# A third tensor of batch 0 (q of heads 2 and 3) through the hardware queue as fp32 rows, cast on chip, with the start's order planned anew

## The chip, the cores and the metric

The kernel runs on one core of one Trainium2 chip. The metric is the device time of one execution in microseconds (us), as the median of several runs; lower is better. The profile is one execution recorded by the hardware profiler.

In the names of the engines, PE is TensorE (matmuls; PEld is its weight load), ACT is ScalarE, DVE is VectorE, POOL is GpSimd and SP is SyncE. POOL and SP start DMA transfers: those of POOL go through the software queue (q0 in the profile) and can change the type on the way, those of SP go through the hardware queue (q1) and copy as is. All of them are moved by the core's 16 DMA engines.

## The reference

Two operations, one after the other. First a causal attention with a sliding window of 64 positions, then a feed-forward layer with SiLU:

```python
# q, k, v: (8, 8, 576, 64) float32;  w_in: (512, 2048), w_out: (2048, 512)
scores = (q @ k.transpose(0, 1, 3, 2)) / 8          # head_dim 64
mask = (rel >= 0) & (rel < 64)                      # rel = row - column
attn = softmax(where(mask, scores, -1e9))
x = (attn @ v).transpose(0, 2, 1, 3).reshape(4608, 512)
h = x @ w_in
out = (h * sigmoid(h)) @ w_out                      # (4608, 512) float32
```

## The kernel before, in words

**The work.** Inputs are loaded once and turned to bf16. The attention is done batch by batch (8 batches). Its result goes, transposed, into a tile `bridge`. The feed-forward part works on 9 tiles of 512 tokens: a first layer (L369, out of `bridge` and `w_in_sb`), SiLU on ACT (L375, into tiles `g`), a second layer (L381, out of `g` and `w_out_sb`), a copy out of PSUM (L387) and a store by SP (L391). The first tile, j = 0, is widened to 576 columns, all of batch 0. Its first layer is done in passes: for the feature blocks ft 0 to 7 the columns 0 to 191 (128x192 matmuls), then for the same blocks the columns 192 to 575 (128x384), then ft 8 to 15 in two pieces each.

**Batch 0** has a way of its own, in `add_first_batch`. There are 8 loads of q and k, each of two heads (a *pair* u), in the order of `FIRST_LOADS`: q0 k0 q1 k1 q2 q3 k2 k3. So q1 is the q of heads 2 and 3. Each of them lies in DRAM as 128 rows of 2304 B.

- q0 and k0 come by `load_first` (L232): SP moves 288 KB of fp32 rows into a tile `nat`, and ACT or DVE then casts them into a tile `natb` (`cast_first`, L235).
- The other six come by `load_first_cast` (L229): POOL issues a DMA that casts on the way, 144 KB into `natb`.
- When two pairs of one tensor are there, PE turns them with 18 transposes (`turn_first`, L282) into two PSUM banks, and ACT and DVE lift them into `qt` and `kt` (L289).
- Then come scores with the mask as a bias (L311, L319), exp on ACT (L337), values (L349), a reciprocal (L356), a product (L359) and a transpose into `bridge` (L363) on DVE. There are six such units: three groups g of 192 columns for each half a of the heads. v arrives by POOL (L253), and half of each v tile is shifted to other partitions (L297, L299).

While PE has nothing else to do at the start it runs filler matmuls on an empty tile (`warm`, L595).

**The order.** A planner, `Plan.run`, walks through an event simulation with a cost for every operation, and fixes one order of instructions for every engine at build time. On the chip each engine goes through its own list and waits on semaphores; nothing is reordered. Costs of DMAs enter as `dma=...`: there are two pipes in the planner, one for SP and one for POOL, with a slowdown when both are busy.

**The queues.** POOL's list at the start is: four of the six casting loads, the constant `ident` (L188), the other two, the constant `window` (L193, L195), four v loads (L253), ten loads of w_in (L259: four of 256 columns, then six of 512, in pairs of two row halves), and then, mixed, the rows of batch 1 (L239), w_out (eight loads, L265) and v of batch 1. Every DMA of POOL waits for the one eight before it to have landed, since its semaphores are used in turn. SP's list is q0 and k0, and then nothing until the first store, after 51 us.

**What waits for the weights.** A block ft of the first layer needs its columns of w_in: ft 0 and 1 the first pair of loads, 2 and 3 the second, 4 to 7 the third, and so on. The second layer of tile 0 goes f by f, and f needs w_out load f // 2.

Of the kernel before, what the change touches and what calls it, by code (L numbers as in the profile page):

```python
# [8 lines left out]
FP32 = mybir.dt.float32  # L9
# [5 lines left out]
class Plan:  # L15
# [31 lines left out]
    def run(self):  # L47
        head = {c: 0 for c in self.queues}
        engines = sorted({e for q in self.queues.values() for op in q for e in op["us"]})
        free = {e: 0.0 for e in engines}  # L50
        can = {e: [c for c, q in self.queues.items() if any(e in op["us"] for op in q)] for e in engines}
        table, left = "exp", self.count
        pipe, sent = {True: 2.0, False: 0.0}, []
        events, order = [0.0], []
        while left:
            if not events:
                raise RuntimeError([(c, head[c], q[head[c]]["n"]) for c, q in self.queues.items() if head[c] < len(q)])
            now = self.now = heapq.heappop(events)
            while events and events[0] == now:
                heapq.heappop(events)  # L60
            moved = True
            while moved:
                moved = False
                for e in engines:
                    if free[e] > now:
                        continue
                    best, kept = None, set()
                    heads = [(self.queues[c][head[c]], c) for c in can[e] if head[c] < len(self.queues[c])]
                    for op, c in sorted(heads, key=lambda x: x[0]["first"]):
                        if e == "POOL" and op["dma"] and len(sent) >= 8 and sent[-8] > now:  # L70
                            continue
                        if e not in op["us"] or not self.done(op["deps"]) or (op["gate"] and not op["gate"]()):
                            continue
                        if op["pool"]:
                            idle = [i for i in self.pools[op["pool"]] if i not in kept and self.done(self.banks[i])]
                            if len(idle) < len(op["untils"]):
                                if op["pool"] != "mp":
                                    kept.update(self.pools[op["pool"]])
                                continue
                            idle.sort(key=lambda i: (op["pool"] == "mp" and i in self.pools["pv"],  # L80
                                                     max([u["seen"] for u in self.banks[i]], default=0.0)))
                            op["bank"] = idle[:len(op["untils"])]
                            for i, until in zip(op["bank"], op["untils"]):
                                self.banks[i] = until
                        best = (op, c)
                        break
                    if best is None:
                        continue
                    op, c = best
                    head[c] += 1  # L90
                    us = op["us"][e]
                    if op["table"] and op["table"] != table:
                        table, us = op["table"], us + 1.28
                    end = free[e] = now + us
                    soft = e == "POOL"
                    if op["dma"] is None:
                        op["seen"] = end + op["lat"]
                    elif soft:

                        begin = max(pipe[True], end + 1.4)  # L100
                        pipe[True] = begin + op["dma"] * (1.5 if pipe[False] > begin else 1.0)
                        op["seen"] = pipe[True] + op["lat"] + 1.2
                        sent.append(op["seen"])
                        heapq.heappush(events, op["seen"])
                    else:
                        begin = max(pipe[False], end + 1.0)
                        busy = pipe[True] > begin
                        pipe[False] = begin + op["dma"] * (1.6 if busy else 1.0)
                        if busy:
                            pipe[True] += 0.6 * op["dma"]  # L110
                        op["seen"] = pipe[False] + {"ld0": 1.2, "st": 1.2}.get(c, 3.0)
                    op["at"], op["cls"], op["by"] = now, c, e
                    order.append((op, e))
                    left -= c != "warm"
                    moved = True
                    heapq.heappush(events, end)
                    heapq.heappush(events, op["seen"])
        for op, e in order:
            op["fn"](e)
# [3 lines left out]
def kernel(ctx, tc, q, k, v, w_in, w_out, out):  # L123
    nc = tc.nc
    B, H, S, D = q.shape
# [13 lines left out]
    FIRST_LOADS = [(x[0], int(x[1])) for x in "q0 k0 q1 k1 q2 q3 k2 k3 v0 v1 v2 v3".split()]  # L139
# [20 lines left out]
    nats = [keep.tile([128, 2 * S], BF16, name=f"nat{i}") for i in range(NN)]  # L160
# [15 lines left out]
    p = Plan(  # L176
        {"at": range(4), "pv": range(4, 6), "mp": range(4, 8), "all": range(8)},
        rank=dict(prime=-8, early=-10, one=-9, edge=-8.5, first=-9, dma=-1, ld0=-1, dma0=-8.7, st=-2, silu=-3, out=-2, pv=0, s=1, moe=99, warm=200, turn=2,
                  norm=0, inverse=0, bridge=0, exp=1, mask=1, lift=2, block=2, shift=2, cast=4, rest=3, late=5, clear=9),
        rank0=dict(turn=-6, cast=-6, lift=-5, shift=-4.5, exp=-4, mask=-4, inverse=-3.5, norm=-3, bridge=-3.2),  # L180
        ahead=dict(s=-5.5, exp=-4.6, pv=-5.5, inverse=-4.3, norm=-4.2, bridge=-4.25),
    )
# [42 lines left out]
    def two(u, kk):  # L225
        return (q, k)[kk][0, 2 * u:2 * u + 2].rearrange("h s d -> (h s) d").rearrange("(p m) d -> p (m d)", m=NM0)

    def load_first_cast(w, u, kk):
        nc.gpsimd.dma_start(out=natbs[w][:, 0:S], in_=two(u, kk))  # L229

    def load_first(i, kk):
        nc.sync.dma_start(out=nats[i][:, 0:2 * S].bitcast(FP32), in_=two(0, kk))  # L232

    def cast_first(e, i, w):
        copies[e](out=natbs[w][:, 0:S], in_=nats[i][:, 0:2 * S].bitcast(FP32))  # L235
# [178 lines left out]
    def add_first_batch():  # L414
        got = {}
        for what, u in FIRST_LOADS:
            if what == "v":
                add_v_loads(0, [u], [c_vv[0]])
                continue
            kk = "qk".index(what)  # L420
            w = n_nat[1] % NNB
            n_nat[1] += 1
            if u == 0:
                i = n_nat[0] % NN
                n_nat[0] += 1
                ld = p.add("ld0", {"SP": 0.45}, lambda _, i=i, kk=kk: load_first(i, kk), dma=-0.15 if kk == 0 else 0.7)
                ca = p.add("cast", {"ACT": 0.7, "DVE": 0.56}, lambda e, i=i, w=w: cast_first(e, i, w), [ld])
                nat_free[i] = [ca]
            else:
                ca = p.add("early" if (what, u) in FIRST_LOADS[2:6] else "dma0", {"POOL": 0.6}, lambda _, w=w, u=u, kk=kk: load_first_cast(w, u, kk), dma=0.74)  # L430
            got[what, u] = (w, ca)
            if (what, u ^ 1) not in got:
                continue
            a = u // 2
            ws, loaded = zip(*[got[what, 2 * a + i] for i in range(2)])
            tu = p.add("turn", {"PE": 0.6}, None, [*loaded, c_ident], lat=0.1, pool="all", nb=2)
            tu["fn"] = lambda _, tu=tu, ws=ws: turn_first(tu, ws)
            for i in range(2):
                tu["untils"][i].append(p.add("lift", {"ACT": 0.64, "DVE": 0.75}, lambda e, tu=tu, a=a, kk=kk, i=i:
                                             lift(e, tu, a, kk, i), [tu, c_k[0]]))  # L440
                kq_done[(0, a)] = kq_done.get((0, a), []) + tu["untils"][i]
# [23 lines left out]
    def add_v_loads(b, parts, busy):  # L465
        v_landed.setdefault(b, []).extend(
            p.add("dma", {"POOL": 1.0}, lambda e, part=part: load_v(e, b, part), busy, dma=1.0 if b == 0 else 1.1, lat=MARGIN * (b > 0)) for part in parts)
# [120 lines left out]


    add_first_batch()  # L590
    add_batch_v(0)

# [59 lines left out]
```

The softmax here doesn't subtract the row's maximum and nothing guards it: scores larger than these inputs give would overflow.

## Time and profile before

| what | value |
|---|---|
| time, median of 7 runs | 299.8 us (299.47 to 301.85) |
| profiled execution: its own time | 299.47 us |
| profiled execution: span | 297.7 us |
| PE busy | 286.4 us (96%), 3609 matmuls |
| ACT, DVE, POOL busy | 176.4, 138.3, 117.8 us |
| software queue q0 | 18.07 MB, 65.5% of the 16 DMA engines' span |
| hardware queue q1 | 10.03 MB, 9.5% |
| granted TensorE clock | 1.0 |

So 1.77 us of the profiled execution's own time lie outside its span. The other view that matters is the timeline, which lists instructions in order of time: start, duration, engine, line, operation, tiles, count, and in brackets how long the engine was idle before and what released it. Consecutive instructions of one kind are merged. The DMA view gives for each kind of DMA the KB and the median time from issue to landing. The chain of waits is followed back from the last instruction, and a piece of it that says "DMA" is a stretch in which nothing but that transfer set the time.

### The profile page before, as it was taken

The numbers are of one execution on the slowest core, as the hardware profiler recorded it, in microseconds if no ns is written. First come the engines' busy times: TensorE is split into PE (matmuls) and PEld (weight loads), VectorE is DVE, ScalarE is ACT, GpSimd is POOL, SyncE is SP. The second block draws the span as 40 slices with busy tenths as digits, with TensorE's granted clock in tenths as the row PEclk, the third lists the DMA queues.
The fourth block names the chain that finished last, engine by engine and source line by source line (L and its number), as shares of the span: only waits on it lengthen the run. The fifth ranks groups of instructions, "written<-read, shape, count | busy, mean of one in ns | idle before, by whom it ended". The sixth has DMA issues, their size and how long they took to land.

```text
span 297.7 us, 8484 instructions
## 1 busy us (share of the span) xinstructions
PE 286.4 (96%) x3609; PEld 149.3 (50%) x3641; DVE 138.3 (46%) x340; ACT 176.4 (59%) x340; POOL 117.8 (40%) x175
## 2 busy tenths in 40 slices
PE   8979989899999999999999999999999999999996
PEld 4556645774444544454444544454444544444445
DVE  3772378969985479327931692066006610000000
ACT  4878655786376745675477537743876376216512
POOL 8967976879799989940500000000000000000000
PEclk9999999999999999999999999999999999999999
DMA  8999999999999999982950210011001100010012
GB/s 163 173 201 175 146 166 169 233 121 137 181 165 140 129 178 177 149 84 75 105 48 0 75 53 20 2 40 70 35 0 40 73 35 2 35 72 35 2 70 72
DMA packets 82982, 28.64 MB, mean 96 GB/s; under 512 B 72448, under 2 KB 78208, under 8 KB 82944
## 3 DMA queue, kind: packets, MB, share of 16 engines
q0 software_dynamic: 77184, 18.07, 65.5%
q1 hardware_dynamic: 5760, 10.03, 9.5%
q8 instruction: 28, 0.46, 0.6%
q14 instruction: 10, 0.08, 0.1%
HBM read 36.70 MB, written 9.44 MB: 155 GB/s over the span
## 4 chain that ended last, share of the span: by engine, by line
PE 82%; POOL 8%; DMA 5%; issue 2%; ACT 1%; POOLq 0%; ACTq 0%
PE mp L381 39%; PE mp L369 37%; PE at L331 3%; PE mp L349 3%; DMA w_in_sb<-in_moe_w_in_dram 3%; DMA w_out_sb<-in_moe_w_out_dram 2%; POOL w_in_sb L259 2%; POOL nat L239 2%; POOL vv L253 2%; POOL natb L229 1%; POOL w_out_sb L265 1%; ACT ot L387 0%; ACT g L375 0%; PE at L349 0%; POOL window L193 0%
## 5 line engine op out<-in xcount | busy, mean ns | idle before, releaser
L369 PE MATMUL mp<-bridge,w_in_sb 128*128 128x512 bf16 (+5 forms) x696 | 128.6, 342 | 2.6 <-DMA w_in_sb<-in_moe_w_in_dram 1.0
L381 PE MATMUL mp<-w_out_sb,g 128*128 128x512 bf16 (+2 forms) x576 | 124.3, 367 | 4.5 <-issue 3.2
L375 ACT ACTIVATE g<-mp 128x512 bf16<-128x512 f32 (+5 forms) x174 | 89.6, 524 | 31.5 <-PE mp L369 30.3
L369 PEld LDWEIGHTS <-w_in_sb 128*128 128x128 bf16 x696 | 66.2, 97 | 63.1 <-issue 7.3
L381 PEld LDWEIGHTS <-g 128*128 128x128 bf16 x608 | 56.0, 98 | 61.9 <-issue 1.4
L387 ACT COPY ot<-mp 128x512 f32<-128x512 f32 (+2 forms) x36 | 20.2, 564 | 62.1 <-PE mp L381 42.8
L340 DVE TENSOR_TENSOR e<-e,mask 128x384 bf16<-128x384 bf16 x84 | 26.0, 347 | 49.1 <-ACT e L337 48.6
L337 ACT ACTIVATE e<-at 128x384 bf16<-128x384 f32 x90 | 37.3, 496 | 16.2 <-PE at L331 16.0
L239 POOL DMA_DIRECT2D nat<-in_k_dram x56 | 35.2, 643 | 8.3 <-DMA vv<-in_v_dram 3.9
L253 POOL DMA_DIRECT2D vv<-in_v_dram x32 | 31.9, 1013 | 14.8 <-PE mp L349 13.3
L239 POOL DMA_DIRECT2D nat<-in_q_dram x56 | 34.5, 632 | 4.4 <-DMA w_in_sb<-in_moe_w_in_dram 1.6
L363 DVE STREAM_TRANSPOSE bridge<-ox 128x384 bf16<-128x384 bf16 x48 | 24.7, 552 | 0.0
L246 DVE STREAM_TRANSPOSE kt<-nat 128x576 bf16<-128x576 bf16 x28 | 20.7, 782 | 6.0 <-DMA nat<-in_k_dram 6.0
L246 DVE STREAM_TRANSPOSE qt<-nat 128x576 bf16<-128x576 bf16 x28 | 20.9, 786 | 3.7 <-DMA nat<-in_q_dram 3.4
L359 DVE TENSOR_TENSOR ox<-mp,rc 128x384 bf16<-128x384 f32 x43 | 21.4, 537 | 0.1
L356 DVE RECIPROCAL rc<-mp 128x6 f32<-128x6 f32 x43 | 7.9, 189 | 18.5 <-PE mp L349 17.7
L349 PEld LDWEIGHTS <-e 128*32 128x32 bf16 x1152 | 10.9, 95 | 9.0 <-issue 5.1
L299 DVE COPY vv<-vv 64x576 bf16<-64x576 bf16 (+1 forms) x14 | 7.3, 523 | 14.0 <-DMA vv<-in_v_dram 11.2
L349 PE MATMUL mp<-vv,e 128*32 128x65 bf16 x1032 | 12.6, 194 | 0.2 <-ACT e L337 0.2
L331 PE MATMUL at<-qt,kt 32*128 32x64 bf16 x1008 | 11.6, 190 | 0.0
L331 PEld LDWEIGHTS <-kt 32*128 32x128 bf16 x1008 | 9.3, 92 | 4.3 <-issue 3.3
L337 ACT ACT_TABLE_LOAD x7 | 9.0, 1283 | 0.1
(53 smaller groups left out, 84.3 us busy)
## 6 DMA issues: line engine op xcount, KB each, us to landing
out_dram<-ot SPq DMA_DIRECT2D x35, 256.0 KB, 2.1
vv<-in_v_dram POOLq DMA_DIRECT2D x32, 144.0 KB, 5.1
nat<-in_q_dram POOLq DMA_DIRECT2D x56, 72.0 KB, 3.9
nat<-in_k_dram POOLq DMA_DIRECT2D x56, 72.0 KB, 3.9
w_out_sb<-in_moe_w_out_dram POOLq DMA_DIRECT2D x8, 256.0 KB, 6.6
w_in_sb<-in_moe_w_in_dram POOLq DMA_DIRECT2D x6, 256.0 KB, 7.6
w_in_sb<-in_moe_w_in_dram POOLq DMA_DIRECT2D x4, 128.0 KB, 5.1
natb<-in_q_dram POOLq DMA_DIRECT2D x3, 144.0 KB, 5.1
```

The lines of the kernel that those rows point to most:

```text
L239: nc.gpsimd.dma_start(out=nats[i][32 * h:32 * h + 32].rearrange("p (m x) -> p m x", m=NB), in_=(q, k)[kk][b, 4 * a + h].rearrange("(m p r) ...
L246: nc.vector.transpose(out=to[:, (2 * a + part) * S:(2 * a + part + 1) * S].rearrange("x (m t r) -> x m r t", t=32, r=2), in_=nats[i].rearr ...
L253: queue[e].dma_start(out=vv[b % NV][:, 2 * g0 + 1:2 * g1 + 1:2, 0:D], in_=v[b].rearrange("h s d -> (h s) d").rearrange("(g p) d -> p g d", ...
L331: nc.tensor.matmul(at_six(op["bank"][h])[:, a, x], lhsT=kt[b % NK][r, at:at + 128], rhs=qt[b % NK][r, at:at + 64], start=(s == a == x == 0 ...
L337: nc.scalar.activation(out=es[n % NE], in_=at_six(bank), func=ACTF.Exp, scale=scale)
L340: nc.vector.tensor_mul(es[n % NE], es[n % NE], mask0 if g == 0 else mask)
L349: nc.tensor.matmul(at_pv(bank)[32 * h:32 * h + 32, x, t], lhsT=e_of(b, a, n, h)[:, x, 32 * t:32 * t + 32], rhs=vv[b % NV][:, (4 * a + h) * ...
L359: nc.vector.tensor_mul(oxs[n % NOX], at_pv(bank)[:, :, :, 0:D], rcs[n % NRC].unsqueeze(3).to_broadcast([128, 3, 2, D]))
L363: nc.vector.transpose(out=bridge[:, n0:n0 + 3, 2 * a:2 * a + 2].rearrange("x t s (u i) -> x t s u i", u=2), in_=oxs[n % NOX].rearrange("p ...
L369: nc.tensor.matmul(banks[bank["bank"][0]][:, 0:hi - lo], lhsT=w_in_sb[:, c, ft * 128:(ft + 1) * 128], rhs=bridge[:, (j * TT + lo) // 64:(j ...
L375: nc.scalar.activation(out=gts[gt][:, lo:hi], in_=banks[bank["bank"][0]][:, 0:hi - lo], func=ACTF.Silu)
L381: nc.tensor.matmul(banks[bank["bank"][0]][:, 0:hi - lo], lhsT=gts[gt][:, m * 128:(m + 1) * 128], rhs=w_out_sb[:, f, lo:hi], start=(f == 0) ...
```

## The change

The load of q1 (q, heads 2 and 3, batch 0) is taken from POOL and given to SP: `load_first` gets the pair u as an argument, and the first three entries of `FIRST_LOADS` take that way. The transfer is now 288 KB of fp32 into a `nat` tile, and a cast by ACT or DVE comes behind it. The class "early", which puts four casting loads ahead of `ident` in POOL's list, moves on by one entry, and now holds k1, q2, q3, k2. The planner's costs for loads of the class `ld0` change too: 0.69 each in place of -0.15 and 0.7, no slowdown beside POOL's transfers, and 0.5 us in place of 1.2 from the end of the transfer to its being seen.

```diff
                         begin = max(pipe[False], end + 1.0)
-                        busy = pipe[True] > begin
+                        busy = pipe[True] > begin and c != "ld0"
...
-                        op["seen"] = pipe[False] + {"ld0": 1.2, "st": 1.2}.get(c, 3.0)
+                        op["seen"] = pipe[False] + {"ld0": 0.5, "st": 1.2}.get(c, 3.0)
...
-    def load_first(i, kk):
-        nc.sync.dma_start(out=nats[i][:, 0:2 * S].bitcast(FP32), in_=two(0, kk))
+    def load_first(i, u, kk):
+        nc.sync.dma_start(out=nats[i][:, 0:2 * S].bitcast(FP32), in_=two(u, kk))
...
-            if u == 0:
+            if (what, u) in FIRST_LOADS[0:3]:
...
-                ld = p.add("ld0", {"SP": 0.45}, lambda _, i=i, kk=kk: load_first(i, kk), dma=-0.15 if kk == 0 else 0.7)
+                ld = p.add("ld0", {"SP": 0.45}, lambda _, i=i, u=u, kk=kk: load_first(i, u, kk), dma=0.69)
...
-                ca = p.add("early" if (what, u) in FIRST_LOADS[2:6] else "dma0", {"POOL": 0.6}, lambda _, w=w, u=u, kk=kk: load_first_cast(w, u, kk), dma=0.74)
+                ca = p.add("early" if (what, u) in FIRST_LOADS[3:7] else "dma0", {"POOL": 0.6}, lambda _, w=w, u=u, kk=kk: load_first_cast(w, u, kk), dma=0.74)
```

The two programs' lists, laid side by side, differ as follows.

- **SP:** q0, k0, q1 in place of q0, k0.
- **POOL:** k1, q2, q3, k2, `ident`, k3, `window` in place of q1, k1, q2, q3, `ident`, k2, k3, `window`. All that follows keeps its order and stands one place earlier.
- **PE:** 18 fillers before the first turn in place of 15; then the turns of q0/q1, k0/k1 and q2/q3 one after another, two fillers, and the turn of k2/k3, all ahead of the first scores. Before, one filler stood behind the first turn and four behind the second, and the first unit of scores stood ahead of the turn of k2/k3. The six units of scores now come as (g0, a0), (g1, a0), (g0, a1), (g2, a0), two units of values, and the last two. From the first matmul of the first layer on, the list is the same but for the numbers of the PSUM banks.
- **ACT:** a third cast (q1) behind the two, and all four of its lifts ahead of the first exp. Before, three stood there and the fourth between the second and third exp.
- **DVE:** the two mask constants (L206) ahead of the first lift; the product of the second unit ahead of that of (g0, a1). Its later list is the same.

The tiles `nat` that batch 1 and later ones take are one further round the ring of eight.

## The prediction

> **What bounds the kernel now.** I read the page first: PE is busy in nearly every slice of the span, at full clock, and the DMA row is full only at the start.
>
> ```profile
> PE   8979989899999999999999999999999999999996
> PEclk9999999999999999999999999999999999999999
> DMA  8999999999999999982950210011001100010012
> ```
>
> So the time is PE's fixed work plus the gaps in it, and an edit of the start counts only through gaps. The chain of waits says which: until PE takes over at 42.27 us the chain consists of POOL's issues and of two waits for weights.
>
> ```profile
> 5.51 3.95 POOL vv L253 x4
> 9.46 4.12 POOL w_in_sb L259 x6
> ...
> 14.43 1.39 POOL w_in_sb L259 x2
> 15.82 9.00 DMA w_in_sb<-in_moe_w_in_dram
> ...
> 35.47 6.76 DMA w_out_sb<-in_moe_w_out_dram
> 42.23 0.04 issue
> 42.27 1.02 PE mp L381 x4
> ```
>
> The timeline of PE shows the gaps themselves: the first layer starts at 16.33, waits 0.40 for `bridge`, 0.97 for the third pair of w_in loads (until 19.76), then runs without a gap to the second layer, which waits 0.42 and 0.36 for w_out.
>
> ```profile
> 16.33 0.34 PE L369 MATMUL mp<-bridge,w_in_sb 128*128 128x192 bf16 x2
> 17.07 1.73 PE L369 MATMUL mp<-bridge,w_in_sb 128*128 128x192 bf16 x16 [0.40 <-DVE bridge L363]
> 19.76 14.37 PE L369 MATMUL mp<-bridge,w_in_sb 128*128 128x192 bf16 x110 [0.97 <-DMA w_in_sb<-in_moe_w_in_dram]
> ...
> 40.03 1.89 PE L381 MATMUL mp<-w_out_sb,g 128*128 128x512 bf16 x8 [0.42 <-DMA w_out_sb<-in_moe_w_out_dram]
> 42.27 1.02 PE L381 MATMUL mp<-w_out_sb,g 128*128 128x512 bf16 x4 [0.36 <-DMA w_out_sb<-in_moe_w_out_dram]
> ```
>
> Two chains thus meet. The **weights' stream** (POOL's DMAs in their order) sets 19.76 and 42.27. The **attention's start** (loads, turns, exps, 16.33) has 0.97 us of slack against it, and 0.42 + 0.36 = 0.78 more before the end of the kernel feels it. Is the stream held by POOL's issuing or by the DMA engines? POOL's timeline answers:
>
> ```profile
> 9.38 7.15 POOL L259 DMA_DIRECT2D w_in_sb<-in_moe_w_in_dram  x10
> 16.52 1.26 POOL L239 DMA_DIRECT2D nat<-in_q_dram  x2
> 18.26 0.61 POOL L239 DMA_DIRECT2D nat<-in_q_dram  x1 [0.48 <-DMA w_in_sb<-in_moe_w_in_dram]
> 20.00 0.60 POOL L239 DMA_DIRECT2D nat<-in_q_dram  x1 [1.13 <-DMA w_in_sb<-in_moe_w_in_dram]
> ```
>
> It never waits until 16.5, then waits at each DMA for the eighth one before to land: from there the engines hold it. Earlier, the time from issue to landing tells: 3.9 us for the first casting load, 4.9 to 5.4 for the other five, 5.2 to 6.0 for v, 5.1 for the small w_in loads, up to 9.0 for the last. Since a 72 KB load in an idle stretch later lands 2.8 us after its issue, something like 1.4 us of transfers is queued from k1 on. The engines bind nearly from the start, at the rates of these rows (busy shares of the engines, then clock, DMA share and GB/s, counted in bytes written):
>
> ```profile
> 3.00:4.00 1.00, 1.00 (x5) 0.50 (x4) 0.00 (x0) 0.33 (x1) 0.94 (x4) 1.00 1.07 345
> 5.00:6.00 1.00, 1.00 (x18) 0.55 (x17) 0.46 (x2) 0.15 (x1) 0.93 (x3) 1.00 1.04 149
> 7.00:8.00 1.00, 1.00 (x21) 0.70 (x17) 0.75 (x2) 0.64 (x1) 1.00 (x2) 1.00 1.16 177
> ```
>
> **The change, part by part.**
>
> *The stream, removed and added.* POOL loses one issue of 0.56 us. The engines lose a casting load of 147 KB written (295 KB read) and get 295 KB of fp32. In finer slices the hardware queue alone runs at 378 to 396 GB/s between 2.5 and 3.5 us, so 295 KB take about 0.75 us; the casting stream runs at 177, so 147 KB take 0.83 us (the landings of k1 at 6.8 and k3 at 9.8 give 0.75 each). Difference: between 0 and -0.08 us. There may be a little more: at 5 to 6 us the stream is at 149 only, 0.16 us of transfer below the later rate, which a second queue may fill. I take -0.1 us.
>
> Two rules of the Trainium skill bear on this, both in "DMA: Bandwidth & Descriptors". Its section "Issuing engines are not separate DMA queues" speaks against the change: DMAs of all engines run on the same 16 engines, and another issuer saves only the issue. Taken by itself this allows POOL's 0.56 us, all of it if issuing bound. The backlog above says that it doesn't: the ring's wait for the eighth DMA before gives the 0.56 back, since w_in load 7 already stands within 0.1 us of the landing that it waits for (v2, about 13.4, issue at 13.67). The section "Where 436 GB/s comes from" puts the ceiling of the SBUF ports at 435 GB/s, and about 358 on HBM's side. If the written bytes bound, doubling them would cost 147 KB / 435 = 0.34 us; the rows have 345 to 390 written by fp32 and 177 x 2 = 354 read by the casts, so reading binds both alike, and I leave that 0.34 as the upper end. Ends for the stream: -0.56 and +0.34; taken: -0.1.
>
> *Later in the stream.* The same DMAs wait for the same ones, so its shift is handed on: last w_in landing (24.83), 10.4 us of POOL issues without a wait, w_out at 42.23, PE. The order there is unchanged.
>
> *The attention's start, moved.* Nothing of it ends the kernel if it stays within the slack, so I reckon its end.
> - q1: SP issues it at 1.6 (0.37 and 0.42 for the two before). The landings of the hardware loads are 2.9 and 3.3 us after issue, 0.83 apart: 5.3. From 3.75 on it shares the engines with k1, which makes 5.9. The third cast (0.67, as the two of 1.48 for two) ends at 6.0 to 6.7 on ACT, idle there before until 6.10.
> - PE: 15 fillers ended at 5.59; three more of 0.32 make 6.55. So the first turn stands at 6.55 to 6.75 in place of 5.58. Each turn takes 0.65: k0/k1 to 7.9, q2/q3 to 8.6, two fillers to 9.2. k3 is issued at 3.83 in place of 4.38; 5.4 us later is 9.2. With the stream unmoved it lands as before at 9.8. So the turn of k2/k3 begins at X = 9.2 to 9.8 (before, 9.59).
> - From X on: turn 0.65, six units of scores at 0.71, six of values at 0.41 make 7.4; so PE reaches the first layer at 16.6 to 17.2. ACT: first exp at X + 1.5 = 10.7 to 11.3 (before, 9.70), then 12 exps at 0.385 and a v shift of 0.67, 5.3 us, with no lift between them (0.72 before): table load at 16.0 to 16.6 (before, 16.00), first SiLU 1.43 later at 17.4 to 18.0. The lift taken out of the exps nearly pays for the later start.
> - DVE: the bridge of (g0, a1) at about X + 7.8 = 17.0 to 17.6 (before, 17.01), the last one at X + 11.6 = 20.8 to 21.4 (before, 20.78). It is needed when the second pass begins, about 19.76 + 1.63 = 21.4.
>
> PE has then 16 matmuls until it needs the third w_in pair at 19.7, done by 18.9 to 19.4. So the start is later by 0.3 to 0.9, and the wait of 0.97 shrinks to 0.3 to 0.8: cost nothing. Its cover is that wait; if the start slips further, the 0.78 at w_out take it, and past that it is paid in full.
>
> *At no cost:* the two mask constants (0.50) ahead of the first lift on DVE, since DVE waits for the first turn anyway, and masks are first used after 41; SP has nothing else until 51; fillers replace each other; the bank numbers and the shift in `nat` add no wait, as no tile is wanted again sooner.
>
> *Sum:* 299.47 (the profiled execution) - 0.1 = 299.37; it stood 0.33 below the median of 299.8, so 299.7.
>
> **The rivals.**
> 1. *No change to speak of* (my forecast): 299.4 to 300.1. Chance 0.70.
> 2. *POOL's issuing binds after all*, so all 0.56 us come through: 299.2. For it: the v loads land about as far apart as POOL issues them (1.0), and the small w_in loads too (0.7). Against it: the backlog. 0.13. It too lies within 0.3%, which is 0.9 us, about what a measurement of this kernel can tell from no change.
> 3. *Slower: q1 becomes the load that the start waits for.* Place: the second transpose on PE, behind ACT's third cast; every turn stands behind it in PE's list. Price: the hardware queue's third load gets few turns beside the casting stream, and X moves with it. The last bridge, X + 11.6, passes 21.4 + 0.78 = 22.2 from X = 10.6 on, that is, from q1 landing at about 7.3 rather than 5.9. At 8.5, 1.2 us are paid: 301.0. For it: stores beside loads at 50 to 60 us landed after 6.1 us rather than 2.1. Against it: the queue's 345 to 390 GB/s before POOL's first load, and only one casting load in flight then. 0.12.
> 4. *Something frees more* (the stream gains in both ways, and w_out's wait falls away): 298.8. 0.05.
>
> That the load does not go where it says is excluded: SP's list has it.
>
> **How the numbers follow.** Faster by over 0.3% is rival 4, 0.05; slower is rival 3 and the ends of the costs, 0.14; the rest, 0.81, is within. The range 299.0 to 300.6 takes in rivals 1 and 2, the +0.34, and the beginning of rival 3.
>
> **What would show it.** Right: an ACT cast of three with the third starting near 6; PE's first layer at 16.6 to 17.2; its wait for w_in smaller than 0.97 but still ending within 0.3 of 19.76; w_out waits at about 40 and 42.2. Wrong: 19.76 moved by over 0.4, a first turn later than 7.5, or the wait for w_in gone and one for `bridge` behind it.

## The result, and the profile after

The changed kernel takes 301.79 us (median of 15 runs, 299.90 to 303.06); the kernel before, run beside it, has the median 299.8. The ratio is 1.0052, with a 95% interval of 1.0035 to 1.0069: slower by about 1.6 us. The prediction was no change (299.7, range 299.0 to 300.6). The profiled execution of after took 300.4 us for itself, with a span of 298.6, so it is one of its quicker ones.

The page of after shows no new hole in PE's row and no lower clock; its last digit falls from 6 to 5.

```profile
PE   8989999899999999999999999999999999999995
PEclk9999999999999999999999999999999999999999
DMA  8999999999999999981940210011001100020012
```

At the start, in this execution, PE kept close to the predicted times. In its timeline the first turn (the transposes of L282) stands at 6.76 and the first layer starts at 17.11. The wait for `w_in_sb`, which was to shrink to 0.3 to 0.8, is gone: one of 0.41 for SiLU's `g` and an idle of 0.67 without any semaphore ("issue") stand there. One wait for `w_out_sb` is left, at 47.08.

```profile
6.76 0.69 PE L282 MATMUL at<-ident,natb 128*64 128x128 bf16 x18
...
17.11 1.03 PE L369 MATMUL mp<-bridge,w_in_sb 128*128 128x192 bf16 x8
18.54 1.98 PE L369 MATMUL mp<-bridge,w_in_sb 128*128 128x192 bf16 x22 [0.41 <-ACT g L375]
21.19 13.38 PE L369 MATMUL mp<-bridge,w_in_sb 128*128 128x192 bf16 x98 [0.67 <-issue]
...
47.08 0.59 PE L381 MATMUL mp<-w_out_sb,g 128*128 128x512 bf16 x2 [0.36 <-DMA w_out_sb<-in_moe_w_out_dram]
47.60 0.56 PE L349 MATMUL at<-vv,e 128*32 128x65 bf16 x48
```

The last of these lines stands in before at

```profile
47.52 0.56 PE L349 MATMUL at<-vv,e 128*32 128x65 bf16 x48
```

so PE is 0.08 us behind there. The difference of 0.9 us between the two spans lies elsewhere. The chain of waits ends in both kernels with ACT's copy of the last tile. First before, whose span is 297.7, then after:

```profile
294.90 0.27 ACT ot L387
```

```profile
294.99 0.27 ACT ot L387
```

So up to the last copy only 0.09 us are lost, but from the start of that copy to the end of the span it takes 3.61 us in place of 2.80. The waits of SP's queue (engine and line, what was waited for: us in total, times, longest) have one line that differs. First before, then after; L647 is the end of the program.

```profile
SPq L647 <- DMA out_dram<-ot: 0.3, 1, 0.3
```

```profile
SPq L647 <- DMA out_dram<-ot: 1.2, 1, 1.2
```

The last store lands 1.6 us after its issue in both. In the trace of SP's semaphore instructions the end is a row of nine waits. The second to the ninth take in the eight semaphores that SP's DMAs use in turn (the ring), in their order. Before has 40 such DMAs (2 loads, 38 stores), so its last store is on the eighth. The view of L647 by stretches (durations, first and last start) shows eight waits passing ahead of the landing and one at it:

```profile
L647 SPq EVENT_SEMAPHORE  x8: 28/28/28, 295.6 to 296.5; - x8
```

```profile
L647 SPq EVENT_SEMAPHORE  x1: 28/28/28, 296.8 to 296.8; - x1
```

After has 41, and the last store is on the first of the eight. One wait passes ahead of the landing, and eight pass one after another only behind it:

```profile
L647 SPq EVENT_SEMAPHORE  x1: 28/28/28, 295.7 to 295.7; - x1
```

```profile
L647 SPq EVENT_SEMAPHORE  x8: 28/28/28, 296.9 to 297.7; - x8
```

That is theory T (tail) of the expectations below: the change costs 0.8 us at the end because it adds one DMA.

But 0.8 us is 0.0027 of the time, and the ratio was 1.0052. A second theory has the rest: rival 3 of the prediction, q1's landing late in other executions than the profiled one. The expectations call it S (start) at first and L (late q1) later; in the last two of them S stands for the semaphores. Of the 16 executions of after, four had a mean granted clock of 0.991 to 0.994, which a start like the one above does not explain. The lower clock is not all of it either: the twelve others have a median of 301.3.

### The profile page after: what moved, and what is told of

The parts are those of the page before. It is cut to its first block, busy times and chain, and to the rows that moved or that the text cites. A ratio compares the mean times of both kernels' runs of the same rounds, so it can differ in the third digit from the quotient of the medians.

```text
span 298.6 us, 8485 instructions
## 1 busy us (share of the span) xinstructions
PE 286.5 (96%) x3609; PEld 149.4 (50%) x3641; DVE 139.4 (47%) x340; ACT 176.8 (59%) x341; POOL 117.4 (39%) x174
## 4 chain that ended last, share of the span: by engine, by line
PE 81%; DMA 8%; POOL 7%; issue 3%; ACT 1%; POOLq 0%; ACTq 0%
PE mp L381 38%; PE mp L369 37%; PE mp L349 3%; PE at L331 3%; DMA w_in_sb<-in_moe_w_in_dram 3%; DMA w_out_sb<-in_moe_w_out_dram 3%; POOL vv L253 2%; POOL nat L239 2%; DMA vv<-in_v_dram 2%; POOL w_out_sb L265 1%; POOL natb L229 1%; POOL w_in_sb L259 0%; ACT ot L387 0%; ACT g L375 0%; PE at L349 0%
## 5 line engine op out<-in xcount | busy, mean ns | idle before, releaser
L239 POOL DMA_DIRECT2D nat<-in_k_dram x56 | 34.6, 632 | 10.6 <-DMA vv<-in_v_dram 5.5
L239 POOL DMA_DIRECT2D nat<-in_q_dram x56 | 35.1, 644 | 3.8 <-DMA nat<-in_k_dram 1.6
L356 DVE RECIPROCAL rc<-mp 128x6 f32<-128x6 f32 x43 | 8.0, 190 | 18.8 <-PE mp L349 18.2
```

What stands on the lines that cost most here:

```text
L239: nc.gpsimd.dma_start(out=nats[i][32 * h:32 * h + 32].rearrange("p (m x) -> p m x", m=NB), in_=(q, k)[kk][b, 4 * a + h].rearrange("(m p r) ...
```

## The experiments

Each is timed against before on the same chip; the chip differs between groups. Where a load changes its queue or its place in POOL's list, the planner also orders PE, ACT and DVE anew at the start, so those runs change more than the load. Splits, added or missing fillers and the unread load leave the other lists as they were; the traces show it. "Split" means this edit of `store`, which adds N DMAs to SP and moves nothing else (N = 1, 7 or 8):

```diff
-        nc.sync.dma_start(out=out[r0:r0 + 128, lo:hi], in_=ots[ot][:, lo:hi])
+        if 4 <= 4 * j + m < 4 + N:
+            nc.sync.dma_start(out=out[r0:r0 + 128, 0:256], in_=ots[ot][:, 0:256])
+            nc.sync.dma_start(out=out[r0:r0 + 128, 256:512], in_=ots[ot][:, 256:512])
+        else:
+            nc.sync.dma_start(out=out[r0:r0 + 128, lo:hi], in_=ots[ot][:, lo:hi])
```

### The end of the program

**Before, one store split (41 DMAs).**

> The kernel before, with one store of tile 1 split into two halves of 128 KB, so that SP issues 41 DMAs in place of 40, as in the changed kernel; the loads and the start are those of before. Theory T (tail): SP's eight semaphores are used in turn, and at the end SP waits for them one after another, so a count of 41 puts the last store on the first of them, and seven waits stand behind its landing. T expects the end of the span 0.8 to 0.9 us later behind the same last store, and a time 0.8 us over before (ratio about 1.0028). Theory S (start): the loss comes from the loads and turns of batch 0; S expects a ratio of 1.000.

Measured: 301.04 us, ratio 1.0042 (1.0023 to 1.0061). From the start of the last copy (295.60) to the end of the span (299.3): 3.70 us. SP's wait is that of after:

```profile
SPq L651 <- DMA out_dram<-ot: 1.2, 1, 1.2
```

**Before, eight stores split (48 DMAs), the control.**

> The control: the kernel before with eight stores split, 48 DMAs of SP, so that the last store is again on the eighth semaphore. T and S both expect a ratio of 1.000 within 0.001; anything else is the price of splitting stores, to be taken off the other runs.

Measured: 300.04 us, ratio 0.9998 (0.9981 to 1.0015), 2.81 us at the end. One DMA more costs what eight more don't, so it is the place of the last store in the ring of eight and not the number of stores.

### The rest: the start

**After, seven stores split (48 DMAs)**, and **after again**, beside it.

> The changed kernel with seven stores split, 48 DMAs of SP: the start is that of the changed kernel, the last store is back on the eighth semaphore. T expects the profile's end as in before, about 1.9 us behind the end of the last copy, and the time 0.85 us below the changed kernel; if T is all, the ratio to before is 1.000 to 1.001. S expects it to stay at about 1.005. If both act, about 1.002 to 1.003.

> The changed kernel once more beside the others, on the same chip. T and S both expect a ratio of about 1.005 as measured before; its profile is a second execution, which shows whether the first 43 us vary from execution to execution (first turn near 6.8, first layer near 17.1, last w_out wait near 47 in the first one).

Measured: 300.69 us, ratio 1.0014 (0.9996 to 1.0032) with the end mended; 301.41, ratio 1.0046 (1.0032 to 1.006) for after as it is. So the end carries some 0.003 of the ratio; what is left is not larger than its interval in this comparison alone. Both profiles, however, happened to catch the late q1 that the first one had not. ACT's cast of q1 begins at 5.89 in the first profile of after; in the version with the split it is at

```profile
7.84 0.67 ACT L235 CAST natb<-nat 128x576 bf16<-128x576 f32 x1 [2.95 <-DMA nat<-in_q_dram]
```

and in the second profile of after at

```profile
8.44 0.67 ACT L235 CAST natb<-nat 128x576 bf16<-128x576 f32 x1 [3.42 <-DMA nat<-in_q_dram]
```

SP issues q1 at 1.65 in each; it landed 4.2, 6.2 and 6.8 us later. In the traces the packets of the casting stream begin at 3.5 to 3.7, and the last of q1's starts among them, at 5.5, 7.5 and 8.1. PE's timeline in the last of the three shows what it does to the start:

```profile
5.78 0.24 PE L282 MATMUL at<-ident,natb 128*64 128x128 bf16 x1
9.16 1.17 PE L282 MATMUL at<-ident,natb 128*64 128x128 bf16 x17 [3.14 <-ACT natb L235]
...
20.90 1.06 PE L369 MATMUL mp<-bridge,w_in_sb 128*128 128x192 bf16 x8
```

The second transpose stands until 9.16, and every turn is behind it. The first layer comes at 20.90 rather than 17.11. That is 3.8 us, while q1 was only 2.55 us later. The table by stretches (busy shares of PE, PEld, DVE, ACT, POOL, then granted clock, DMA share, GB/s) has the other part: from 8 us on the clock is at half.

```profile
6.00:8.00 2.00, 0.02 (x1) 0.00 (x0) 0.95 (x3) 0.00 (x0) 2.00 (x3) 1.00 1.14 205
8.00:10.00 2.00, 0.84 (x16) 0.84 (x18) 0.00 (x0) 0.73 (x2) 2.00 (x3) 0.50 1.68 181
10.00:12.00 2.00, 2.00 (x43) 2.00 (x37) 1.40 (x2) 1.59 (x3) 1.73 (x4) 0.50 2.42 156
12.00:14.00 2.00, 2.00 (x25) 1.07 (x21) 0.77 (x2) 0.89 (x2) 1.50 (x3) 0.50 1.96 175
```

In slices of half a microsecond it stays at 0.5 for some 6.8 us there (from 8.0 on), and for 3.4 us (from 9.5 on) in the version with the split. The mean clocks of the two executions, 0.989 and 0.994, are just that: half of 6.8 us and of 3.4 us, over 300. The 22 executions with the split fall into eight with a clock of 0.994 or less (median 301.28) and fourteen above (300.25; before beside it 300.07). So most of what is left here goes with the low clock.

**Which load is late?** In the next version k3, which the start needs last, takes the third place on SP, and q1 is back with POOL; seven stores are split, as in the two after it.

```diff
-            if (what, u) in FIRST_LOADS[0:3]:
+            if (what, u) in (("q", 0), ("k", 0), ("k", 3)):
...
-"early" if (what, u) in FIRST_LOADS[3:7]
+"early" if (what, u) in FIRST_LOADS[2:6]
```

> As the changed kernel with seven stores split (the end as before), but the third load of the hardware queue is k3, wanted last, in place of q1, wanted first; q1 is POOL's first load again. Theory L (late q1): the hardware queue's third load lands 4 to 7 us after its issue, because it shares the engines with POOL's casting loads, and only where the first turn waits for it does that cost. L expects the third load to land as late as before, at 6 to 8.5, but ahead of its turn near 9.5, so no gap on PE ahead of the first turn beyond 0.4, the clock at 0.998 or above in nearly all executions, and a ratio to before of 0.998 to 1.000. Rival C (a third fp32 load costs the engines more, whoever waits for it): the ratio stays at about 1.0014 to 1.002 as with q1.

Measured: 300.39 us, ratio 1.0023 (1.0002 to 1.0043). A miss for the theory that only the wait for q1 costs. In its profile k3 landed 6.5 us after its issue and was ready well in time, but POOL's own casting loads took longer too: 5.4 us for q1 (3.9 in before) and 6.4 to 6.7 for the others (4.9 to 5.4). So the third load is late whichever it is, and the casting loads are late with it. That it delays them does not follow: in the control above, which has only q0 and k0 on SP, k0 landed 4.3 us after its issue (3.3 in before) and the casting loads took 4.5 for the first and 5.6 to 6.1 for the others.

**Nobody waits for the third load.** Before, with q1's rows loaded once more as fp32, as SP's third load, into a tile of its own that nothing reads; q1 itself comes by POOL as before. Seven stores split.

```diff
+    extra = keep.tile([128, 2 * S], BF16, name="extra")
...
         nc.sync.dma_start(out=nats[i][:, 0:2 * S].bitcast(FP32), in_=two(0, kk))
+        if kk:
+            nc.sync.dma_start(out=extra[:, 0:2 * S].bitcast(FP32), in_=two(1, 0))
```

> Before, with one load added that nobody reads: q1's rows also come as fp32, 288 KB, as the third load of SP's queue, into a tile of its own; q1 itself still comes by POOL. Seven stores are split in two so that SP has 48 DMAs and the last store waits on the eighth semaphore. Theory C (a third fp32 load beside the casting stream delays the casting loads, whoever waits for it): the casting loads land 5.5 to 6.5 us after issue rather than 3.9 to 5.4, first turns and the weights late, ratio 1.003 to 1.006 (there are also 295 KB read in addition, some 0.8 us of engine time). Theory L (only the wait for q1 itself costs): just the 0.8 us of additional transfer on the weights' stream, of which the stream's waits of 0.97 and 0.78 hide some: ratio 1.000 to 1.002.

Measured: 301.0 us, ratio 1.0031 (1.0011 to 1.005). The DMA view (KB each, median us from issue to landing) shows both again with nobody waiting: the unread load takes 5.6, and the casting loads 6.1 and 6.4, in place of the 5.1 of both in before (5.8 and 5.9 in the control).

```profile
natb<-in_q_dram POOLq DMA_DIRECT2D x3, 144.0 KB, 6.1
natb<-in_k_dram POOLq DMA_DIRECT2D x3, 144.0 KB, 6.4
...
extra<-in_q_dram SPq DMA_DIRECT2D x1, 288.0 KB, 5.6
```

Here the weights' stream was later too (its last w_in load was waited for until 26.64 rather than 25.11), since 295 KB are added and none taken away. So this run shows that such a load, its bytes included, costs time even if nobody waits for it, but its ratio is not the price of the change, and how much of the casting loads' delay is its doing stays open.

**Cover for PE, and a later stream.** Two attempts to mend the start, each with q1 third on SP and seven stores split. In the first, nine more fillers stand in the first turn. In the second, POOL sends k1 first and the other casting loads only after the constants, about 0.9 us later.

```diff
-    def turn_first(op, ws):
+    def turn_first(op, ws, late=False):
+        for _ in range(9 * late):
+            nc.tensor.matmul(banks[op["bank"][0]][:, 0:384], lhsT=blank, rhs=blank.unsqueeze(1).to_broadcast([128, 3, 128]),
+                             start=True, stop=True)
```

```diff
-        rank=dict(prime=-8, early=-10, ... dma0=-8.7, ...
+        rank=dict(prime=-8, early=-8.4, ... dma0=-8.3, ...
```

> As the changed kernel with seven stores split, with nine more filler matmuls ahead of the first turn, which then begins at about 9.4 in every execution, whether q1 is late or not. Theory L with the clock: a part of the loss is that PE stands idle for 2 to 3 us ahead of a late q1 and its clock then falls to 0.5 for 4 to 6 us. It expects the clock at 0.998 or above in all executions, the first layer 10.35 us behind the first turn as in the first profile of the changed kernel (19.7), and the last copy 1 to 1.5 us later than in before (295.9 to 296.4), with little spread: ratio 1.003 to 1.005. Without a part of the clock, the late profiles would owe all to q1 itself, and the first layer would stand 10.7 to 11.7 us behind the turn here too (20.1 to 21.1).

> As the changed kernel with seven stores split, with POOL's second casting load and the later ones issued behind the two constants, about 0.9 us later, so that q1 shares the engines with k1 alone at first. L expects q1 to land at 5.0 to 6.0, hardly ever later, the clock full, and the weights' stream up to 0.5 us later; ratio 1.000 to 1.002. If sharing with the casting loads is not why q1 is late, it lands at 5.9 to 8.5 as before and the low clock stays in about a third of the executions.

Measured: 300.76 us, ratio 1.0029 (1.0013 to 1.0045) with the fillers; 299.73, ratio 1.0002 (0.9982 to 1.0023) with the later stream. The fillers missed their expectation: the low clock became rarer (three of 22 executions at 0.994), but in the profile it came all the same, at 21.2 us, behind an idle of 1.54 us within the first layer that no semaphore explains. Holding the stream back gave a median at before's, but the interval doesn't part it from the version without the hold (1.0014), and its slowest execution still had q1 5.8 us after issue, beside k1 alone until POOL's next issue at 2.75, and an idle of 2.65 us within the first turn. Both are inconclusive as cures.

**What an idle PE costs by itself.** Before, with seven of the fillers ahead of the first turn left out; loads and order stay.

```diff
     def warm(op):
+        n_warm[0] += 1
+        if 8 < n_warm[0] <= 15:
+            return
```

> Before, with the seven fillers ahead of its first turn left out, so that PE idles from about 3.5 to the first turn at 5.6 while loads, order and everything else stay. It prices the idle PE by itself. Theory K (an idle of some 2 us at the start lets the granted clock fall to 0.5 for 4 us or more, and the attention's start is then late by 2 us or so): a clock of 0.995 or less in most executions, first layer 1 to 2.5 us later, ratio 1.001 to 1.005. Rival (the clock fell in the late executions for another reason, and an idle PE costs nothing here): full clock, first layer within 0.3 us of 16.3, ratio 0.999 to 1.001.

Measured: 300.62 us, ratio 1.0028 (1.0018 to 1.0038). The price is that of theory K, its mechanism only in part: four of the 22 executions have a clock of 0.995 or less, and the other eighteen still have a median of 300.52. The profile shows why. The turns run at half pace: 18 transposes take 1.17 us at 7.31 and at 9.80, 0.69 in the first profile of after. The granted clock reads 1.0 there, but the first record of it in this trace is at 11.96 (5.20 in before), and the profile shows what lies ahead of the first record as 1.0. From 12.06 on the last turn runs at full pace. So here the clock did not fall at first; it was released later. (Behind some 1.6 us of idle that end at 17.9 it then falls as well, to 0.5 from 18.8 to 22.2.) The first layer is at 20.45, 4.1 us later than in before.

```profile
7.31 1.17 PE L282 MATMUL at<-ident,natb 128*64 128x128 bf16 x18
8.41 1.14 PE L600 MATMUL mp<-blank 128*128 128x384 bf16 x3
9.35 0.53 PE L600 MATMUL at<-blank 128*128 128x384 bf16 x1
9.80 1.17 PE L282 MATMUL mp<-ident,natb 128*64 128x128 bf16 x18
```

The Trainium skill, in "TensorE: Matmul & The Clock Gate", Part 1, has such a rule: PE begins at half its clock and is released by about 3.4 us of steady work. That agrees with the fillers of before, which follow one another in 0.32 us until 4.8 and in about 0.17 after; the clock records begin at 4.0 to 6.7 in the other profiles that have one. The page puts the fall at idle times of over about 3.4 us; here 0.7 to 3.1 us were enough in five profiles (and 0.97, 1.94 and 2.65 us in others, before's own 0.97 among them, were not), so the measurement decides. In length the falls agree with it: 3.4 us, and once twice that. So do their places: in the records each of the five falls begins a whole number of 3.41 us behind the first record of its execution (1, 1, 2, 4 and 5 times). So a fall comes at the next step of a grid that lies differently in each execution. What decides at a step is not shown by the idle time in it: 1.1 us of idle came ahead of the fall at 18.3, while 1.9 us in one step (4.0 to 7.4 in the version with the later stream) brought none.

### An earlier issue, and the ring again

If the third load is late because POOL's stream is already under way at 1.65, an earlier issue should help. ACT has a hardware queue of its own (q10 in these profiles, 0.29 MB) and nothing to do at 0.7. In the first version q1 goes there (seven stores split), in the second the same without any split.

```diff
-        nc.sync.dma_start(out=nats[i][:, 0:2 * S].bitcast(FP32), in_=two(u, kk))
+        (nc.scalar if u else nc.sync).dma_start(out=nats[i][:, 0:2 * S].bitcast(FP32), in_=two(u, kk))
```

> As the changed kernel with seven stores split, with q1 issued by ACT's own hardware queue at 0.74, beside SP's q0, in place of 1.65 behind q0 and k0. L expects q1 to be moved before POOL's first load reaches the engines, all three by about 5.0, k0 perhaps 0.5 later; the first turn near 6.6, the clock full, ratio 0.999 to 1.001. A rival, that the third fp32 load itself is too much, expects one of the three to land as late as q1 did (7.8 to 8.4) in a third of the executions, with the low clock.

> After with one further change: q1 is issued by ACT's hardware queue as ACT's first instruction, instead of by SP as its third. SP then has 40 DMAs, so that the last store waits on the eighth semaphore as in before, with no store split. Theory T (the end's order of waits costs 0.85 us, and a q1 issued late behind the casting stream costs the rest): span end 2.7 to 2.8 us behind the start of the last copy, q1 landing 3.4 to 3.7 after issue as in the split version; ratio to before 0.997 to 1.001, best guess 0.999. Rival (the gain of the split version came from its split stores, or was chance): ratio 1.002 or more.

Measured: 299.49 us, ratio 0.9992 (0.9973 to 1.0012), and 301.16, ratio 1.0036 (1.0021 to 1.0051). q1, issued at 0.74, landed 3.5 to 3.6 us later in the profiles of both, so q1 is in time in both; the split ought not to have mattered. The waits of SP's queue in the second say what went wrong:

```profile
SPq L647 <- DMA out_dram<-ot: 1.2, 1, 1.2
```

The late end is back (3.68 us from the last copy's start), although SP has 40 DMAs. Either ACT's DMA takes one of the same eight semaphores, so that there are 41 all the same, or the split itself does something. Two more versions tell it apart. In one, k0 goes by ACT and q1 second by SP, without a split (41 in all) and with seven (48):

```diff
-        nc.sync.dma_start(out=nats[i][:, 0:2 * S].bitcast(FP32), in_=two(u, kk))
+        (nc.scalar if kk else nc.sync).dma_start(out=nats[i][:, 0:2 * S].bitcast(FP32), in_=two(u, kk))
```

> After with one further change: k0, not q1, is issued by ACT's hardware queue, and q1 is the second load of SP's queue, so it is issued at about 1.2 rather than 1.65. SP has 40 DMAs. If an early issue of all three loads is what counts (all are ahead of POOL's stream): all three land within 4 us, first turn at 6.6 to 7.2, ratio 0.998 to 1.001, as with q1 on ACT's queue. If it is the second queue for q1 itself that counts: q1 lands 4.5 us or more after its issue in some executions, ratio 1.001 to 1.003, with several executions at a clock of 0.994 or less.

> The version with k0 on ACT's hardware queue and q1 second on SP's, with seven stores split in two, so that SP and ACT together have 48 DMAs of the hardware rings. Theory S (ACT's DMA takes the same eight semaphores in turn as SP's; so 41 in all put the last store on the first semaphore in the two versions without splits): span end 2.7 to 2.8 us behind the start of the last copy, and the ratio falls by 0.0028 from 1.0008 to 0.9980 (0.9965 to 0.9995). Rival D (the split stores themselves, or the issue on ACT, make the difference between the two versions with q1 on ACT's queue, not the semaphore): the end unchanged at 3.6 us, ratio 1.000 to 1.002.

Measured: 300.15 us, ratio 1.0008 (0.9997 to 1.0019) with 41; 299.2, ratio 0.9978 (0.9966 to 0.999) with 48, where 0.9980 was expected. The ends take 3.63 and 2.77 us. The ring counts ACT's DMA. The traces say so directly: ACT's load stands on the first of the eight semaphores, SP's first load on the second, and with 41 the last store is again on the first. And the version with 48 is faster than both kernels: none of its 22 executions has a clock under 0.995 (though none of the 43 of before beside it has either), and in its profile q1 is cast in one go with q0 and no wait for weights is left on PE.

```profile
4.42 1.48 ACT L235 CAST natb<-nat 128x576 bf16<-128x576 f32 x2 [1.97 <-DMA nat<-in_q_dram]
```

```profile
16.89 0.91 PE L369 MATMUL mp<-bridge,w_in_sb 128*128 128x192 bf16 x8
18.33 5.96 PE L369 MATMUL mp<-bridge,w_in_sb 128*128 128x192 bf16 x45 [0.53 <-ACT g L375]
```

The other version is before with k0 by ACT: 40 in all, no split. It is not k0's queue alone that differs: the planner gave PE, ACT and DVE another order at the start (k0's cast goes to DVE, for one); POOL's list is that of before.

> Before with one change: k0 is issued by ACT's hardware queue instead of as SP's second; q1 stays a casting load of POOL. SP and ACT together have 40 DMAs. Theory S: no store is split and 40 is a multiple of eight, so the end is as in before (2.7 to 2.8 us behind the last copy's start). k0 is issued 0.45 us earlier; the first turn still waits for q1 by POOL at 5.6, so ratio 0.9985 to 1.0005. If an issue by ACT takes a semaphore of its own and not one of the eight, SP's 39 DMAs put the last store on the seventh: the end 0.1 to 0.5 us later or earlier, ratio 0.999 to 1.002.

Measured: 300.55 us, ratio 1.0026 (1.0011 to 1.004). Its end is that of before, 2.78 us and a wait of 0.3, as the ring of eight says. The ratio is a miss. In its profile the stream is late (the last w_in load was waited for until 26.23, and w_out for 1.11 us at 43.59), and the last copy begins at 296.12. But that wait ended at 26.06 in the version with one split, whose start is that of before, so one profile does not tell a later stream from its spread. Why the ratio is over 1, by the new order or by k0's queue, stays open.

## Why the prediction was wrong

- **"SP has nothing else until 51", at no cost: wrong.** The step counted the issue of the added DMA and what runs beside it, not what it does to those behind it in the ring. It shifts every later store of SP by one semaphore, and the last one from the eighth to the first. Cost in the profiles: 3.6 to 3.7 us at the end in place of 2.7 to 2.8, in each of the five with 41 DMAs in all and in none of the eleven with 40 or 48. The pairs that differ only in it give 0.0030 to 0.0044 of the ratio (1.0042 against 0.9998, 1.0046 against 1.0014, 1.0036 against 0.9992, 1.0008 against 0.9978). That is the larger part of the 0.0052.
- **q1 "shares the engines with k1, which makes 5.9": a size that holds for one execution.** In the five profiles with q1 third on SP it landed 4.2, 4.5, 5.8, 6.2 and 6.8 us after its issue at 1.65. The landing was taken from the two loads before it plus one transfer beside k1; what is beside it in fact is the casting stream, and how fast it gets through differs from execution to execution. In the four versions that issue all three loads by 1.2, the last of their packets starts at 4.6 to 4.9. The point from which rival 3 decides, 7.3, is 5.65 us after the issue, and three of the five lie past it. The 0.12 given to rival 3 was too little; its price (1.2 us for 8.5) was also short: landing at 8.41 came with a last copy 2.7 us late, and the sum had no term for a lower clock.
- **"At no cost" for the start: wrong in those executions.** In the first profile it held: the first layer at 17.11 (16.6 to 17.2 predicted), PE 0.08 us behind at 47.6. The waits that paid for it were not those foretold, though. The third pair of w_in landed at 18.9 rather than 19.7, so no wait for it was left, the idle of 0.67 stood there instead, and the one w_out wait came at 47.08 rather than at about 40 and 42.2. With the first layer at 19.28 and 20.90 the last copy begins at 296.56 and 297.57, 1.7 and 2.7 us behind before's profile. The price of this part over all executions is what remains with the end mended, 0.0014 with an interval that reaches 1; that the lateness costs is seen in its executions with the low clock, 1.0 us slower than the others, and agrees with 1.0014 against 0.9978, where the queue of k0, q1's place and the order planned from these differ together.
- **The stream, -0.1: too small in the first profile.** There the last w_in load landed at 24.06 and not at 24.83; POOL's lead was taken back at 14.07 by a wait of 0.32 us for v, as the text had it of the ring. But over all profiles POOL's wait for that load ends between 25.1 and 26.2 with q1 on POOL (the version with an added load aside) and between 24.3 and 26.3 with a third load taken from it. So whatever the stream gains is smaller than its own spread.
- **The first turn, right by luck:** 6.76 (6.55 to 6.75). The sum took 0.32 us for each further filler. In before's own profile a filler takes that only until its clock is released at 5.20, and 0.17 behind it (7.48 to 7.98). In the first profile of after the release happened to come at 6.59; in the second it came at 4.60, and the same 18 fillers were done for a first turn at 5.78.
- **Right:** issuing not the bound (rival 2). The saved issue of 0.56 us did not come through: POOL waited for a landing at 14.07 already.

What stays open: how much of the remaining 0.0014 to 0.0024 (1.0014 as measured with the end mended; 1.0052 less 0.0028, the 0.85 us of the end) is the idle PE, how much the granted clock and how much later casting loads, and what decides at a step of the clock's grid. There is a rival that no experiment here varies: in six of the sixteen profiles, the first of after among them, PE stands idle for 0.7 to 1.6 us between 15 and 22 us with no semaphore to wait for. Each time the trace has a 16 KB transfer of an instruction queue (q8) that ended 1.3 to 1.5 us before PE went on, and two of the five falls of the clock came behind such an idle.

## What to carry to other kernels

A DMA added to SP's or ACT's queue can move the last store to another semaphore of the ring; look at what SP waits for at the end of the program, and choose the number of hardware DMAs, over all queues, so that the last store is the last that is waited for. A load that the start depends on should be issued before the casting stream begins, if need be from another engine's queue; here a third one behind it landed anywhere between 4.2 and 6.8 us after its issue. One profile shows one execution: where a landing has no slack, look at it in several before its mean goes into a sum.

## What was not expected of the hardware

- The wait at the end of the program goes through the eight semaphores of the hardware DMAs one after another, SP's and ACT's together: 0.8 to 0.9 us between the best and the worst place of the last store that were tried.
- The granted clock fell to 0.5 for 3.4 us (6.8 in one execution) in five profiles, each time during or soon after an idle PE of 0.7 to 3.1 us: at 8.0, 9.5, 18.3, 18.8 and 21.2 us, always a whole number of 3.41 us behind the first clock record.
- A 288 KB load on the hardware queue, third behind two others, landed between 4.2 and 6.8 us after an issue at 1.65. In the four versions that issued all three by 1.2, each landed 3.4 to 4.0 us after its issue.
